# Slot mixture on one core: one stacked matmul per output tile, with the slot weights prepared ahead of the second expert layer

## The chip, the cores and the metric

One Trainium2 chip, one of its cores. The metric is the device time of one execution in microseconds; a change is judged by the medians of runs of both kernels on the same chip.

## The reference

Attention over learned states feeds a dense layer pair, and that feeds a soft mixture of experts, whose end is what the change touches. `x` has 4608 tokens (8 batches of 512 tokens and 32 state rows) of 512 features, `phi` has 32 slots, 4 for each of 8 experts.

```python
logits = x @ phi                                  # 4608 x 32
d = softmax(logits, axis=0)                       # over the tokens
slot_input = (d.T @ x).reshape(8, 4, 512)
for e in range(8):
    h = np.maximum(slot_input[e] @ w1[e], 0.0)    # 512 -> 1024
    slot_out[e] = h @ w2[e]                       # 1024 -> 512
c = softmax(logits, axis=1)                       # over the slots
return (c @ slot_out.reshape(32, 512)).astype(np.float32)
```

## The kernel before, in words

Eight batches `b` run through attention and the dense layers, and a ninth block `B` holds the 256 state rows. For each the kernel keeps its logits, transposed, in `LT` (512 tokens a batch, in 128 columns) or `LTs` (the state rows). After the last block comes the tail, from line 864 on. It takes the slot inputs (`SI`), the first expert layer (lines 900 to 912: 16 weight slices of 1 MB, 64 matmuls into two PSUM tiles `h1`), and then what the change touches:

- **csoft** (lines 660 to 677) turns the logits in `LT` into the softmax weights of the slots: transpose, maximum, subtraction, exponential, sum, reciprocal, a multiplication on POOL, transpose back.
- **csplit** (lines 679 to 688) spreads these weights for the output matmuls. `pick` (lines 916 to 918) selects one token tile of 128 and copies its 32 slot rows into 64 output rows, so that two batches lie one above the other in a PSUM tile `X` of 128 rows. ScalarE rounds both copies to `fp32r` (a float32 read at reduced precision by TensorE, in one pass), and DVE puts the rounding remainder into the first 32 rows of each 64. Four tiles `LC`, one for each pair of batches, and one `LCs`.
- **hTD** (lines 924 to 934): the first layer's output, transposed and laid on a block diagonal.
- **slot_out(dh)** (lines 943 to 961), for each half `dh` of 256 output columns: for each expert, 8 float32 matmuls with 32 stationary columns, which write four 32-row strips of `SO`. Then the four strips are summed by a matmul with `R` (which also repeats the 32 slot rows four times) into `SR`. ScalarE writes its rounding, DVE the remainder, to `so[0]` and `so[1]`. `SO` and `SR` share one PSUM buffer (pool `psE`, tag `E`).
- **combine(dh)** (lines 963 to 988): nine blocks, in the order 0 to 5, B, 6, 7, with 4 token tiles (2 for B), 34 a half. A tile is two `fp32r` matmuls (line 975), one against `so[0]` (rounding and remainder of the weights at once) and one against `so[1]`. DVE and ScalarE take turns at the eviction; even tiles lie in the three buffers of `psH`, odd ones in the two of `psX`, which `csplit` and `hTp` use as well. A block's 512 KB leave by one DMA on SP's queue; those of B by 8 small ones from POOL.

Lines 990 to 999 set the order of emission: `slot_out(0)` whole, then the splits, then `slot_out(1)` and `combine(0)` in turns by the string `CFG["so"]` (`s` is one expert, `c` one block), then what is left of both and `combine(1)`. A scheduler at build makes the order on each engine from this: of the instructions whose inputs its own estimate has ready, it takes the one emitted first. `group` (lines 121 to 129) keeps a list of matmuls together in that order, by putting all but the first 2000 places forward.

SBUF places are handed on by `give` and `take`: as soon as a weight slice is used up, its place gets the next load (all on SP's queue in this stretch). Four places of the first layer's slices are kept back (`kept`, line 900) for `ct`, `LC`, `hTD` and `so`, in this order. `so` is zeroed by four DVE instructions (lines 936 to 940).

Of the kernel before, what the change touches and what calls it, by code (L numbers as in the profile page):

```python
# [7 lines left out]
F32 = mybir.dt.float32  # L8
F32R = mybir.dt.float32r
U32 = mybir.dt.uint32  # L10
ACTF = mybir.ActivationFunctionType
ALU = mybir.AluOpType
# [1 line left out]
PSUM = bass.MemoryType.PSUM  # L14


CFG = dict(hp=2000, att7=(3, 5, 6, 7, 8, 10), og=1, n3=1, n3m=10, wS=['DP', 'AD', 'AD', 'AD', 'AD', 'DP', 'AD', 'DD', 'AD', 'AD', 'AD', 'AD', 'AD', 'AD', 'AD', 'AD'], xsm=13, k0=5, rg=6, spg=0, att0=6, att=7, V0=(2, 6, 10), Vn=(0, 4, 10), Vx=12, wn='H', wsev='adad', conv=(4, 8, 9, 11, 12, 13, 19, 21, 24, 26, 28, 32, 36, 40, 44, 48, 52, 56, 60), todo=[1, 1, 1, 2, 0, 0, 0, 3, 0, 0, 2, 2, 1, 1, 0, 0], E0=2, E=1, sm=1, tqB=(5, 9, 13), GP=10, pe=(3,), psH=3, gtpX=(0, 7), tq0=(13, 15), keep=(2, 3, 4, 5), x2=(1, 1), natm=1, warm=14, bounce7=(0, 3), split=1, wt=4, so='ssccsccccccsss', smm=(1, 2, 3, 4, 5, 6, 9), tqv=(), tqvm=0, first='x', apath=2, f32c=1, place=1, attm=(3, 6, 7, 8, 9, 12), subPm=True, loDm=False, bounce=(0, 1, 2, 3), bq=('s', 's'), xq='s', nat=((1, 11), (2, 2), (2, 3), (2, 11), (3, 2), (3, 4), (3, 9), (4, 2), (4, 3), (4, 9), (5, 2), (5, 3), (5, 9), (6, 2), (6, 4), (6, 9)), subP=(1,), mulD=(), loD=(), qlag=0, gv0='EEEEEEEEEEEEEEEE', gv='EEEEEEEEEEEEEEEE', gvS='BBBBBBBBBBBBBBBB')


@with_exitstack  # L20
def kernel(
# [14 lines left out]
    nc = tc.nc  # L36
    B = xs.shape[0]
    NS = 32 * B
    scale = 0.125
# [5 lines left out]
    const = pool("const", 1)  # L45
# [4 lines left out]
    small = pool("small", 2)  # L50
    psH = pool("psH", CFG["psH"], space=PSUM)
    psE = pool("psE", 1, space=PSUM)
    psV = pool("psV", 1, space=PSUM)
    psX = pool("psX", 5 - CFG["psH"], space=PSUM)
    dram = pool("dram", 1, space=bass.MemoryType.DRAM)

    cst_t = const.tile([128, 260], F32, name="cst_t")
    ident = cst_t[:, 0:128]
    R = cst_t[:, 128:256]
    R4 = cst_t[:, 128:160]  # L60
    blk = cst_t[:, 256:260]
# [8 lines left out]
    wp = const.tile([128, NM, 32], F32, name="wp", tag="wp")  # L70
    XS = const.tile([128, 4, NS], F32, name="XS", tag="XS")
    acc = const.tile([128, 2048], F32, name="acc", tag="acc")
    NL = (B + 1) // 2
    LT = const.tile([128, 128 * B], F32, name="LT")
    LTs = const.tile([64, 128], F32, name="LTs")
    spare = const.tile([128, 1024], F32, name="spare", tag="spare")
    eS = const.tile([128, 512], F32, name="eS", tag="eS")
# [38 lines left out]
    mm = nc.tensor.matmul  # L116
# [4 lines left out]
    def group(calls, after=()):  # L121

        first = mm(**calls[0])  # L123
        for i in after:
            tc.add_manual_dep(first.ins, i.ins.name, SYNC, reason="side by side")
        with tc.high_priority(CFG["hp"]):
            for c in calls[1:]:
                e = mm(**c)  # L128
                tc.add_manual_dep(e.ins, first.ins.name, ORDER, reason="side by side")

    def act(out, in_, func=ACTF.Copy, **kw):
        return nc.scalar.activation(out=out, in_=in_, func=func, **kw)  # L132
# [258 lines left out]
    def ntok(b):  # L391
        return 512 if b < B else NS

    wS = {}
# [281 lines left out]
                                op=ALU.mult)  # L676
        nc.vector.transpose(out=L, in_=t)

    def csplit(parts, C):

        np_ = 64 * len(parts)
        X = psX.tile([128, 512], F32, tag="X", name="cX")[0:np_, 0:C.shape[1]]
        for q, (L, n) in enumerate(parts):
            for t in range(n // 128):
                mm(out=X[64 * q:64 * q + 64, 128 * t:128 * t + 128], lhsT=pick[0:n // 4, t, :], rhs=L, start=True, stop=True)
        act(C, X)
        for p in range(32, np_, 64):
            nc.vector.tensor_tensor(out=C[p:p + 32], in0=X[p:p + 32], in1=C[p:p + 32], op=ALU.subtract)

    def diag(t, stride, nk, first):  # L690

# [9 lines left out]
    def take(place, name, dt=F32):  # L701

        ts = [p.tile([128, n], dt, name=name, tag=tag) for p, tag, n in place]
        return ts, [t[:, c:c + 512] for t in ts for c in range(0, t.shape[1], 512)]
# [82 lines left out]
    todo = [lambda i=i: conv_win(i) for i in range(2, 8)] + [lambda i=i: conv_wo(i) for i in range(8, 16)]  # L787

    sm = None
    vg = None  # L790
    for b in range(B + 1):
# [6 lines left out]
        for m in range(NM):  # L798
# [12 lines left out]
            if b == 1 and m == CFG["E0"]:  # L811
                for k in range(4):
                    estep(0, k)
                sm = smblock(0)
            if b > 0 and m % 4 == CFG["E"]:
                if m >= 4:
                    estep(b, m // 4 - 1)
                elif b > 1:
                    estep(b - 1, 3)
                    sm = smblock(b - 1)  # L820
# [46 lines left out]
    sm = smblock(B)  # L867
# [13 lines left out]
    tail4 = run["tail"].rearrange("p (a k x) -> p a k x", a=4, k=4)  # L881
# [3 lines left out]
    for i in range(4):  # L885
        for jj in range(4):
            mm(out=SI[32 * jj:32 * jj + 32, :], lhsT=PT[:, jj, 32 * i:32 * i + 32],
               rhs=where["wo", i][1][jj], start=(i == 0), stop=(i == 3))
# [11 lines left out]
    kept, got = [], 0  # L900
    h1 = [psX.tile([128, 512], F32, tag="X", name=f"h1_{i}") for i in range(2)]
    for i in range(16):
        e, hf = divmod(i, 2)
        place, w = where["w1", i]
        for kt in range(4):
            mm(out=h1[hf][32 * kt:32 * kt + 32, :], lhsT=XD[e // 4][:, kt, 32 * (e % 4):32 * (e % 4) + 32], rhs=w[kt],  # L906
               start=(e == 0), stop=(e == 7))
# [5 lines left out]

    ct_place = kept.pop(0)
    ct, = take(ct_place, "ct")[0]
    pick = tail4[:, 1, 0:2].rearrange("p a (b x) -> p (a b) x", b=2)
    for t in range(4):
        nc.vector.tensor_scalar(out=pick[:, t, :], in0=R[:, 0:64], scalar1=blk[:, t:t + 1], scalar2=None, op0=ALU.mult)
    csoft(LTs, 128, 64, SIs)
    csoft(LT, 128 * B, 128, ct)  # L920
    free.append(ct_place)
    LC = take(kept.pop(0), "LC", F32R)[1]
    LCs = const.tile([64, 256], F32R, tag="wp", name="LCs")
    hTD_t, = take(kept.pop(0), "hTD")[0]
    hTD = hTD_t.rearrange("p (k x) -> p k x", k=8)
    nc.gpsimd.memset(hTD, 0.0)
    hTp = psX.tile([128, 8, 32], F32, tag="X", name="hTp")
    for hf in range(2):
        s = run["tail"][:, 1536 * (1 - hf):1536 * (1 - hf) + 512]
# [3 lines left out]
    act(diag(hTD_t, 256, 8, 0),  # L933
        hTp.rearrange("p k (e i) -> p k e i", i=4), ACTF.Relu)

    so = take(kept.pop(0), "so", F32R)[1]
    for t in so:
        nc.vector.tensor_scalar(out=t.rearrange("p (a b) -> p a b", a=2),
                                in0=cst_t[:, 0:256].unsqueeze(1).to_broadcast([128, 2, 256]),
                                scalar1=0.0, scalar2=None, op0=ALU.mult)  # L940
    so = [so[0:2], so[2:4]]

    def slot_out(dh):
        dc = slice(256 * dh, 256 * dh + 256)
        SO = psE.tile([128, 256], F32, tag="E", name="SO")
        for e in range(8):
            place, w = where["w2", 8 * dh + e]
            for ft in range(8):
                c = 32 * (ft % 4)
                mm(out=SO[c:c + 32, :], lhsT=hTD[:, ft, 32 * e:32 * e + 32],  # L950
                   rhs=w[ft // 2][:, 256 * (ft % 2):256 * (ft % 2) + 256], start=(e == 0 and ft < 4), stop=(e == 7 and ft >= 4))
            give(place)
            yield
        SOs = run["tail"][:, 1024 + 256 * dh:1280 + 256 * dh]
        act(SOs, SO)
        SR = psE.tile([128, 256], F32, tag="E", name="SR")
        mm(out=SR, lhsT=R, rhs=SOs, start=True, stop=True)
        for q in range(2):
            p, p2 = slice(64 * q, 64 * q + 64), slice(64 * q, 64 * q + 32)
            act(so[0][q][p, dc], SR[p])  # L960
            nc.vector.tensor_tensor(out=so[1][q][p2, dc], in0=SR[p2], in1=so[0][q][p2, dc], op=ALU.subtract)

    def combine(dh):
        dc = slice(256 * dh, 256 * dh + 256)
        n_ev = 0
        for b in list(range(B - 2)) + [B, B - 2, B - 1]:
            T = ntok(b) // 128
            place = next(p for p in free if p[0][2] >= 256 * T)
            free.remove(place)
            o = take(place, "o")[0][0][:, 0:256 * T].rearrange("p (t d) -> p t d", t=T)  # L970
            for t in range(T):
                q, p, L = (b % 2, slice(0, 128), LC[b // 2]) if b < B else (0, slice(0, 64), LCs)
                ps = (psH, psX)[n_ev % 2].tile([128, 256], F32, tag="HX"[n_ev % 2], name="ops")
                for i in range(2):
                    mm(out=ps, lhsT=L[p, 128 * t:128 * t + 128], rhs=so[i][q][p, dc], start=(i == 0), stop=(i == 1))  # L975
                if n_ev % 2:
                    act(o[:, t, :], ps)
                else:
                    nc.vector.tensor_copy(out=o[:, t, :], in_=ps)  # L979
                n_ev += 1  # L980
            if b < B:
                dma(out=out[544 * b:544 * b + 512, dc].rearrange("(t p) d -> p t d", p=128), in_=o)
            else:
                for bb in range(B):
                    t, q = divmod(bb, 4)
                    (nc.gpsimd.dma_start if CFG["og"] else dma)(out=out[544 * bb + 512:544 * bb + 544, dc], in_=o[32 * q:32 * q + 32, t, :])  # L986
            free.append(place)
            yield

    drain(slot_out(0))  # L990
    csplit([(LTs, NS)], LCs)
    for i in range(NL):
        csplit([(LT[:, 128 * b:128 * b + 128], 512) for b in range(2 * i, min(2 * i + 2, B))], LC[i])
    s1, c0 = slot_out(1), combine(0)
    for x in CFG["so"]:
        step(s1 if x == "s" else c0)
# [42 lines left out]
```

## Time and profile before

| | us |
|---|---|
| median of 3 runs (lowest to highest) | 540.88 (540.31 to 540.95) |
| the profiled execution, its own time | 540.54 |
| its span in the profile | 537.7 |
| TensorE matmuls busy | 481.8 (90% of the span) |
| DVE busy | 395.4 (74%) |
| ScalarE busy | 256.0 (48%) |
| POOL busy | 239.8 (45%) |

How to read it: the span is what the profiler saw from the first to the last instruction; the execution's own time lies 2.84 us above it. The shares are means over stages that differ, so the stage around the change is read on its own below. In the rows, PE is TensorE, PEld its weight loads, DVE VectorE, ACT ScalarE, POOL GpSimd, SPq and POOLq queues that issue DMAs; L950 is line 950. ACT shows L132, the line of its helper, and groups of matmuls show L123 and L128. A float32 matmul leaves two records, an `fp32r` one leaves one.

### The profile page before, as it was taken

Reading aid. Unit: us, or ns where it says so; the run is one execution under the profiler, and the core shown is the slowest. Engines: PE = TensorE matmul, PEld = TensorE weight load, DVE = VectorE, ACT = ScalarE, POOL = GpSimd, SP = SyncE. Lnnn points to the kernel's source line nnn. Section 1 sums busy time; section 2 is a strip of 40 time slices with the busy share of each in tenths; the row PEclk is TensorE's granted clock in tenths of the full one; section 3 lists DMA queues with packets and bytes.
Section 4 is the critical chain, followed back from the end, with each engine's and each line's share of the span. In section 5 each row is a group of like instructions: output and inputs, shape, how many; then the busy total and the mean of one; then the engine's idle time right before and its main releaser. Section 6 shows DMA issues by size and latency. Waiting matters only on the chain.

```text
span 537.7 us, 9910 instructions
## 1 busy us (share of the span) xinstructions
PE 481.8 (90%) x3757; PEld 273.0 (51%) x3757; DVE 395.4 (74%) x728; ACT 256.0 (48%) x508; POOL 239.8 (45%) x230
## 2 busy tenths in 40 slices
PE   4476999999987999999999999999997997999992
PEld 2132455665534555455455455456466683356481
DVE  2999989777578679969969979977964762345260
ACT  2343476576555456456455455455444462023152
POOL 0775667665317366465555555646471000110032
PEclk9686799999999999999999999999998999899996
DMA  8998082457378488789789878879797988996379
GB/s 314 419 402 325 1 293 100 157 177 197 117 227 322 110 296 289 240 251 276 283 219 274 276 222 265 285 221 349 260 324 217 364 338 306 388 419 249 118 254 294
DMA packets 40223, 140.30 MB, mean 261 GB/s; under 512 B 4336, under 2 KB 12912, under 8 KB 28272
## 3 DMA queue, kind: packets, MB, share of 16 engines
q1 hardware_dynamic: 38496, 131.81, 71.2%
q0 software_dynamic: 1680, 7.87, 4.4%
q8 instruction: 29, 0.48, 0.3%
q14 instruction: 18, 0.15, 0.1%
HBM read 98.24 MB, written 39.32 MB: 256 GB/s over the span
## 4 chain that ended last, share of the span: by engine, by line
PE 60%; DVE 18%; DMA 13%; ACT 3%; issue 2%; SPq 2%; POOL 0%; POOLq 0%; DVEq 0%; ACTq 0%
PE h L434 22%; PE F L123 5%; DMA gdr<-gD 4%; PE E L123 4%; PE V L123 4%; PE SO L950 4%; DMA nat<-gD 4%; PE h L442 4%; DMA nat<-gdr 3%; PE ops L975 3%; PE h L906 3%; DVE win L160 3%; PE gtp L512 2%; DVE win L158 2%; DVE v L384 2%
## 5 line engine op out<-in xcount | busy, mean ns | idle before, releaser
L434 PE MATMUL h<-a,v 128*128 128x512 f32 x744 | 200.3, 412 | 5.0 <-DVE nat L486 2.2
L464 POOL TENSOR_TENSOR c<-c 128x512 f32<-128x512 f32 x128 | 135.6, 1064 | 100.4 <-ACT c L132 99.9
L434 PEld LDWEIGHTS h<-a,v 128*128 128x128 f32 x744 | 133.9, 191 | 85.1 <-issue 28.2
L132 ACT ACTIVATE c<-h,half 128x512 f32<-128x512 f32 x128 | 87.8, 688 | 99.1 <-PE h L434 66.6
L486 DVE SCALAR_TENSOR_TENSOR g<-h,c 128x512 f32<-128x512 f32 x112 | 75.2, 672 | 29.8 <-POOL c L464 29.7
L521 DVE STREAM_TRANSPOSE gD<-g 128x512 f32<-128x512 f32 x108 | 75.6, 703 | 1.6
L132 ACT ACTIVATE v<-V 128x512 fp32r<-128x512 f32 x62 | 37.0, 597 | 29.5 <-DVE v L384 14.8
L384 DVE TENSOR_TENSOR v<-V,v 128x512 fp32r<-128x512 f32 x62 | 42.1, 679 | 10.5 <-ACT v L132 9.7
L123 PE MATMUL V<-win,st_t 64*32 64x512 f32 x64 | 35.1, 629 | 9.8 <-POOL win L168 6.5
L128 PE MATMUL V<-win,st_t 64*32 64x512 f32 x448 | 38.3, 630 | 0.0
L123 PE MATMUL F<-nat,dN 128*32 128x512 f32 x54 | 26.9, 601 | 4.5 <-DMA nat<-gdr 2.9
L123 PE MATMUL E<-g,wp 128*32 128x512 f32 x56 | 29.2, 604 | 0.7 <-DVE g L486 0.7
L128 PE MATMUL E<-g,wp 128*32 128x512 f32 x168 | 29.6, 604 | 0.0
L128 PE MATMUL F<-nat,dN 128*32 128x512 f32 x162 | 27.2, 601 | 0.0
L986 POOL DMA_DIRECT2D out_dram<-o x16 | 7.9, 501 | 42.8 <-DVE o L979 37.2
L442 PE MATMUL h<-XSh,v 128*128 128x256 f32 x128 | 26.4, 298 | 0.2 <-ACT nat L132 0.2
L979 DVE COPY o<-ops 128x256 f32<-128x256 f32 x34 | 13.6, 423 | 15.8 <-PE ops L975 15.4
L623 DVE SCALAR_TENSOR_TENSOR acc<-acc,al,F 128x512 f32<-128x512 f32 x28 | 20.7, 739 | 5.7 <-PE F L128 5.5
L320 POOL TENSOR_TENSOR a<-att,a 128x512 fp32r<-128x512 f32 x14 | 18.1, 1305 | 13.4 <-ACT a L132 13.4
L975 PE MATMUL ops<-so,LC 128*128 128x256 f32 x128 | 23.3, 308 | 0.2
L442 PEld LDWEIGHTS h<-XSh,v 128*128 128x128 f32 x128 | 21.2, 197 | 4.1 <-issue 1.9
L264 POOL TENSOR_TENSOR att<-att,m 128x512 f32<-128x512 f32 x14 | 15.1, 1081 | 18.3 <-DVE m L263 15.6
(239 smaller groups left out, 780.9 us busy)
## 6 DMA issues: line engine op xcount, KB each, us to landing
gdr<-gD SPq DMA_DIRECT2D x100, 256.0 KB, 4.8
nat<-gdr SPq DMA_DIRECT2D x25, 1024.0 KB, 5.5
w<-in_w_dram SPq DMA_DIRECT2D x24, 1024.0 KB, 8.8
xn<-in_xn_dram SPq DMA_DIRECT2D x8, 1024.0 KB, 7.7
out_dram<-o SPq DMA_DIRECT2D x16, 512.0 KB, 5.4
xs<-in_xs_dram SPq DMA_DIRECT2D x7, 1024.0 KB, 7.7
w<-in_w_dram POOLq DMA_DIRECT2D x5, 1024.0 KB, 9.5
wb<-in_win_dram SPq DMA_DIRECT2D x4, 1024.0 KB, 11.7
```

The source lines that it names most:

```text
L123: first = mm(**calls[0])
L128: e = mm(**c)
L132: return nc.scalar.activation(out=out, in_=in_, func=func, **kw)
L384: nc.vector.tensor_tensor(out=lo[:, G, :], in0=V[G], in1=hi[:, G, :], op=ALU.subtract)
L434: mm(out=h, lhsT=v[:, G, f], rhs=a[:, G, :], start=(k == 0), stop=(k == 5))
L442: mm(out=h, lhsT=w[:, j, :], rhs=x[:, j, :], start=(k == 0), stop=(k == 11))
L464: nc.gpsimd.tensor_tensor(out=c, in0=c, in1=c, op=ALU.mult)
L486: gI[b, m] = nc.vector.scalar_tensor_tensor(out=g, in0=h, scalar=1.0, in1=c, op0=ALU.max, op1=ALU.min)
L521: nc.vector.transpose(out=gd[:, :, :, m4, :].rearrange("p c a i -> p a c i"), in_=gT[b, m].rearrange("p (a c i) -> p a c i", a=4, i=32))
L623: nc.vector.scalar_tensor_tensor(out=a, in0=a, scalar=al, in1=F, op0=ALU.mult, op1=ALU.add)
L950: mm(out=SO[c:c + 32, :], lhsT=hTD[:, ft, 32 * e:32 * e + 32], rhs=w[ft // 2][:, 256 * (ft % 2):256 * (ft % 2) + 256], start=(e == 0 and f ...
L975: mm(out=ps, lhsT=L[p, 128 * t:128 * t + 128], rhs=so[i][q][p, dc], start=(i == 0), stop=(i == 1))
```

## The change

Three things, and a new order string (an entry of `CFG`, line 17).

1. Each batch has its own weights tile of 128 rows: rounding in rows 0 to 31, remainder in 32 to 63, rounding again in 64 to 95 and in 96 to 127. The slot rows are one tile: rounding in rows 0 to 63, remainder in 64 to 95, zeros in 96 to 127. One matmul over all rows gives the three products of a token tile. `pick` has 128 columns instead of 64. The additional weights tiles lie in the place of `eS` and in three quarters of the place of `so`.
2. The splits are emitted ahead of `hTD` and of the second layer; `hTD` takes the last of the four kept places instead of the third.
3. The 8 matmuls of an expert in `slot_out` are emitted as a `group`. The zeroing of `so` is gone; a ScalarE write with scale 0 makes the zero rows.

```diff
-so='ssccsccccccsss'
+so='cscscscscscscscs'
...
-    def csplit(parts, C):
-        np_ = 64 * len(parts)
-        X = psX.tile([128, 512], F32, tag="X", name="cX")[0:np_, 0:C.shape[1]]
-        for q, (L, n) in enumerate(parts):
-            for t in range(n // 128):
-                mm(out=X[64 * q:64 * q + 64, 128 * t:128 * t + 128], lhsT=pick[0:n // 4, t, :], rhs=L, start=True, stop=True)
+    def csplit(L, n, C):
+        X = psX.tile([128, 512], F32, tag="X", name="cX")[:, 0:n]
+        for t in range(n // 128):
+            mm(out=X[:, 128 * t:128 * t + 128], lhsT=pick[0:n // 4, t, :], rhs=L, start=True, stop=True)
         act(C, X)
-        for p in range(32, np_, 64):
-            nc.vector.tensor_tensor(out=C[p:p + 32], in0=X[p:p + 32], in1=C[p:p + 32], op=ALU.subtract)
+        nc.vector.tensor_tensor(out=C[32:64], in0=X[32:64], in1=C[32:64], op=ALU.subtract)
...
-    LC = take(kept.pop(0), "LC", F32R)[1]
-    LCs = const.tile([64, 256], F32R, tag="wp", name="LCs")
+    LC = take(kept.pop(0), "LC", F32R)[1] + [const.tile([128, 512], F32R, tag="eS", name="LCe")]
+    so = take(kept.pop(0), "so", F32R)[1]
+    LC += so[1:]
+    so = so[0]
+    LCs = const.tile([128, 256], F32R, tag="wp", name="LCs")
+    for b in range(B):
+        csplit(LT[:, 128 * b:128 * b + 128], 512, LC[b])
+    csplit(LTs, NS, LCs)
     hTD_t, = take(kept.pop(0), "hTD")[0]
...
-            for ft in range(8):
-                c = 32 * (ft % 4)
-                mm(out=SO[c:c + 32, :], lhsT=hTD[:, ft, 32 * e:32 * e + 32],
-                   rhs=w[ft // 2][:, 256 * (ft % 2):256 * (ft % 2) + 256], start=(e == 0 and ft < 4), stop=(e == 7 and ft >= 4))
+            group([dict(out=SO[32 * (ft % 4):32 * (ft % 4) + 32, :], lhsT=hTD[:, ft, 32 * e:32 * e + 32],
+                        rhs=w[ft // 2][:, 256 * (ft % 2):256 * (ft % 2) + 256],
+                        start=(e == 0 and ft < 4), stop=(e == 7 and ft >= 4)) for ft in range(8)])
...
-        for q in range(2):
-            p, p2 = slice(64 * q, 64 * q + 64), slice(64 * q, 64 * q + 32)
-            act(so[0][q][p, dc], SR[p])
-            nc.vector.tensor_tensor(out=so[1][q][p2, dc], in0=SR[p2], in1=so[0][q][p2, dc], op=ALU.subtract)
+        act(so[0:96, dc], SR[0:96])
+        act(so[96:128, dc], SR[96:128], scale=0.0)
+        nc.vector.tensor_tensor(out=so[64:96, dc], in0=SR[64:96], in1=so[64:96, dc], op=ALU.subtract)
...
-                for i in range(2):
-                    mm(out=ps, lhsT=L[p, 128 * t:128 * t + 128], rhs=so[i][q][p, dc], start=(i == 0), stop=(i == 1))
+                mm(out=ps, lhsT=L[:, 128 * t:128 * t + 128], rhs=so[:, dc], start=True, stop=True)
```

## Rows read from the trace of the kernel before

**Rows 1.** The head of the page.

```profile
span 537.7 us, 9910 instructions
```

**Rows 2.** Windows: stretch, us, busy PE, PEld, DVE, ACT, POOL; PEclk, DMA share, GB/s.

```profile
477.40:485.00 7.60, 7.60 (x133) 4.43 (x132) 1.66 (x2) 0.76 (x2) 0.60 (x1) 1.00 1.02 414
485.00:490.30 5.30, 4.71 (x55) 3.99 (x51) 2.96 (x5) 1.96 (x4) 0.00 (x0) 1.00 1.02 422
493.00:513.50 20.50, 20.50 (x169) 9.59 (x168) 7.04 (x16) 3.45 (x9) 2.04 (x4) 1.00 0.30 96
513.50:536.00 22.50, 14.24 (x93) 11.98 (x92) 8.72 (x22) 10.45 (x28) 5.87 (x12) 0.84 0.96 310
530.00:536.00 6.00, 0.00 (x0) 0.00 (x0) 0.00 (x0) 0.00 (x0) 0.00 (x0) 0.50 1.05 345
```

**Rows 3.** Timeline of SP's queue, merged: start, us, what; the last weight loads.

```profile
431.91 45.33 SPq L714 DMA_DIRECT2D w<-in_w_dram  x23
```

**Rows 4.** The chain that ended last, in order of time: start, us, what.

```profile
478.01 7.06 PE SO L950 x128
...
490.35 0.43 PE ops L975 x2
490.78 1.51 PE cX L685 x16
...
493.07 1.86 PE SO L950 x32
...
499.12 0.56 PE SO L950 x4
499.68 0.43 PE ops L975 x2
...
512.99 0.55 PE SO L950 x2
...
515.12 2.17 PE ops L975 x15
```

**Rows 5.** The same chain: matmuls with 128 stationary columns.

```profile
447.17 1.09 PE warm L574 x8
...
475.54 1.90 PE hTp L932 x16
```

**Rows 6.** Groups from 475 to the end, shapes apart: busy us, mean ns of one.

```profile
L979 DVE COPY o<-ops 128x256 f32<-128x256 f32 x34 | 13.6, 423 | 15.8 <-PE ops L975 15.4
L132 ACT ACTIVATE o<-ops 128x256 f32<-128x256 f32 x34 | 12.8, 383 | 20.4 <-PE ops L975 19.5 <-DMA out_dram<-o 0.2
...
L688 DVE TENSOR_TENSOR LC<-cX,LC 32x512 fp32r<-32x512 f32 x8 | 5.5, 690 | 8.1 <-ACT LC L132 8.0
...
L132 ACT ACTIVATE LC<-cX 128x512 fp32r<-128x512 f32 x4 | 2.4, 597 | 4.1 <-PE cX L685 4.1
```

**Rows 7.** Timeline of the tail: start, us, engine, line, operation.

```profile
468.74 1.81 POOL L926 MEMSET hTD<- 128x2048 f32 x1 [7.26 <-DMA w<-in_w_dram]
...
470.27 1.55 DVE L938 TENSOR_SCALAR so<-cst_t 128x512 fp32r<-128x512 f32 x4
...
478.03 1.25 DVE L677 STREAM_TRANSPOSE LT<-ct 128x1024 f32<-128x1024 f32 x1 [2.08 <-POOL ct L675]
...
492.44 0.42 DVE L961 TENSOR_TENSOR so<-SR,so 32x256 fp32r<-32x256 f32 x1
...
496.91 0.40 SPq L982 DMA_DIRECT2D out_dram<-o  x1
...
513.58 0.38 ACT L132 ACTIVATE tail<-SO 128x256 f32<-128x256 f32 x1 [1.16 <-PE SO L950]
...
515.15 0.38 ACT L132 ACTIVATE so<-SR 64x256 fp32r<-64x256 f32 x1
```

**Rows 8.** DMA view of 497 to 502 in 40 slices: busy tenths.

```profile
DMA  0000001899999999998200000000000000000000
```

**Rows 9.** Windows, as rows 2, over the slot inputs and the first layer.

```profile
450.00:460.00 10.00, 7.12 (x64) 2.71 (x60) 2.69 (x10) 1.68 (x5) 0.52 (x1) 1.00 0.79 276
460.00:470.00 10.00, 10.00 (x80) 3.09 (x81) 3.02 (x6) 0.21 (x1) 1.65 (x2) 0.83 1.02 428
```

More of the change, by code (lines that the diff above doesn't have):

```diff
@@ L14 @@
 PSUM = bass.MemoryType.PSUM
-CFG = dict(hp=2000, att7=(3, 5, 6, 7, 8, 10), og=1, n3=1, n3m=10, wS=['DP', 'AD', 'AD', 'AD', 'AD', 'DP', 'AD', 'DD', 'AD', 'AD', 'AD', 'AD', 'AD', 'AD', 'AD', 'AD'], xsm=13, k0=5, rg=6, spg=0, att0=6, att=7, V0=(2, 6, 10), Vn=(0, 4, 10), Vx=12, wn='H', wsev='adad', conv=(4, 8, 9, 11, 12, 13, 19, 21, 24, 26, 28, 32, 36, 40, 44, 48, 52, 56, 60), todo=[1, 1, 1, 2, 0, 0, 0, 3, 0, 0, 2, 2, 1, 1, 0, 0], E0=2, E=1, sm=1, tqB=(5, 9, 13), GP=10, pe=(3,), psH=3, gtpX=(0, 7), tq0=(13, 15), keep=(2, 3, 4, 5), x2=(1, 1), natm=1, warm=14, bounce7=(0, 3), split=1, wt=4, so='ssccsccccccsss', smm=(1, 2, 3, 4, 5, 6, 9), tqv=(), tqvm=0, first='x', apath=2, f32c=1, place=1, attm=(3, 6, 7, 8, 9, 12), subPm=True, loDm=False, bounce=(0, 1, 2, 3), bq=('s', 's'), xq='s', nat=((1, 11), (2, 2), (2, 3), (2, 11), (3, 2), (3, 4), (3, 9), (4, 2), (4, 3), (4, 9), (5, 2), (5, 3), (5, 9), (6, 2), (6, 4), (6, 9)), subP=(1,), mulD=(), loD=(), qlag=0, gv0='EEEEEEEEEEEEEEEE', gv='EEEEEEEEEEEEEEEE', gvS='BBBBBBBBBBBBBBBB')
+CFG = dict(hp=2000, att7=(3, 5, 6, 7, 8, 10), og=1, n3=1, n3m=10, wS=['DP', 'AD', 'AD', 'AD', 'AD', 'DP', 'AD', 'DD', 'AD', 'AD', 'AD', 'AD', 'AD', 'AD', 'AD', 'AD'], xsm=13, k0=5, rg=6, spg=0, att0=6, att=7, V0=(2, 6, 10), Vn=(0, 4, 10), Vx=12, wn='H', wsev='adad', conv=(4, 8, 9, 11, 12, 13, 19, 21, 24, 26, 28, 32, 36, 40, 44, 48, 52, 56, 60), todo=[1, 1, 1, 2, 0, 0, 0, 3, 0, 0, 2, 2, 1, 1, 0, 0], E0=2, E=1, sm=1, tqB=(5, 9, 13), GP=10, pe=(3,), psH=3, gtpX=(0, 7), tq0=(13, 15), keep=(2, 3, 4, 5), x2=(1, 1), natm=1, warm=14, bounce7=(0, 3), split=1, wt=4, so='cscscscscscscscs', smm=(1, 2, 3, 4, 5, 6, 9), tqv=(), tqvm=0, first='x', apath=2, f32c=1, place=1, attm=(3, 6, 7, 8, 9, 12), subPm=True, loDm=False, bounce=(0, 1, 2, 3), bq=('s', 's'), xq='s', nat=((1, 11), (2, 2), (2, 3), (2, 11), (3, 2), (3, 4), (3, 9), (4, 2), (4, 3), (4, 9), (5, 2), (5, 3), (5, 9), (6, 2), (6, 4), (6, 9)), subP=(1,), mulD=(), loD=(), qlag=0, gv0='EEEEEEEEEEEEEEEE', gv='EEEEEEEEEEEEEEEE', gvS='BBBBBBBBBBBBBBBB')
 @with_exitstack
@@ L72 @@
     acc = const.tile([128, 2048], F32, name="acc", tag="acc")
-    NL = (B + 1) // 2
     LT = const.tile([128, 128 * B], F32, name="LT")
@@ L915 @@
     ct, = take(ct_place, "ct")[0]
-    pick = tail4[:, 1, 0:2].rearrange("p a (b x) -> p (a b) x", b=2)
+    pick = tail4[:, 1]
     for t in range(4):
-        nc.vector.tensor_scalar(out=pick[:, t, :], in0=R[:, 0:64], scalar1=blk[:, t:t + 1], scalar2=None, op0=ALU.mult)
+        nc.vector.tensor_scalar(out=pick[:, t, :], in0=R, scalar1=blk[:, t:t + 1], scalar2=None, op0=ALU.mult)
     csoft(LTs, 128, 64, SIs)
@@ L934 @@
         hTp.rearrange("p k (e i) -> p k e i", i=4), ACTF.Relu)
[L936 to L941, printed above, removed]
     def slot_out(dh):
@@ L971, in combine @@
             for t in range(T):
-                q, p, L = (b % 2, slice(0, 128), LC[b // 2]) if b < B else (0, slice(0, 64), LCs)
+                L = LC[b] if b < B else LCs
                 ps = (psH, psX)[n_ev % 2].tile([128, 256], F32, tag="HX"[n_ev % 2], name="ops")
-                for i in range(2):
-                    mm(out=ps, lhsT=L[p, 128 * t:128 * t + 128], rhs=so[i][q][p, dc], start=(i == 0), stop=(i == 1))
+                mm(out=ps, lhsT=L[:, 128 * t:128 * t + 128], rhs=so[:, dc], start=True, stop=True)
                 if n_ev % 2:
@@ L990 @@
     drain(slot_out(0))
-    csplit([(LTs, NS)], LCs)
-    for i in range(NL):
-        csplit([(LT[:, 128 * b:128 * b + 128], 512) for b in range(2 * i, min(2 * i + 2, B))], LC[i])
     s1, c0 = slot_out(1), combine(0)
```

## The prediction

> **What bounds the kernel now.** I read the page's head first, then the windows over the tail, then the chain of waits and the timeline there; everything that the diff touches runs after 467 us of a 537.7 us span [rows 1]. That execution took 540.54 us, 2.84 more than its span and 0.34 less than the median of the runs shown, 540.88. My sum is a difference to the span, set against the median.
>
> The windows cut the tail into stages [rows 2]. From 477.4 to 485 TensorE is full and the DMA engines are full as well, at 414 GB/s: these are the last weight loads, all issued by 477.3 on SP's queue [rows 3], so nothing that starts later can delay one. From 493 to 513.5 TensorE is busy all the time while DMA stands at 0.30 and 96 GB/s. From 513.5 to 536 DMA is at 0.96, and its last 6 us, at 345 GB/s, have no other work beside them. The output is 9.44 MB (4608 x 512 x 4 bytes); from 513.5 to 536 the queues move 22.5 x 310 = 7.0 MB, so less than 2.5 MB of it had gone by then. So the kernel ends on an output queue that was fed too late, and it was fed late because TensorE was the bound from 493 to 513.5. The last 1.7 us follow the last transfer.
>
> The chain shows why TensorE takes 20.5 us there [rows 4]. The first strips of the second layer (64 calls, 128 records, since a float32 call leaves two) run as one piece in 7.06 us, 0.88 per expert: four 32-column strips share the array. Between 493 and 513.5 the other half's 64 calls are cut into pieces between token tiles. A piece of 4 records takes 0.56 us, while four calls side by side (8 records) are 0.44 in the whole run, so a cut strip pays for four calls when it does two; the chain has 19 such pieces from 493.07 to 513.54, 12.4 us together. A token tile's two matmuls take 0.43 beside a piece, but 0.29 in the run of 15 in 2.17 (0.145 each). A round of one tile and one piece therefore costs 0.14 for the tile and, against those 0.44, 0.12 for the piece more than the same work in runs: about 0.26, say 0.27, for a change over and back.
>
> **The change part by part.**
>
> *Split of the slot weights.* The number of calls stays (32 for the eight blocks and 2 for the states), but each has 128 stationary columns instead of 64, and all go ahead of the second layer. Sixteen records of 64 columns took 1.51 us, 94 ns each [rows 4]. No call of this shape is in the trace; the nearest with 128 stationary and 128 moving columns is the warming one, eight records in 1.09 us, 136 ns [rows 5]. The transposing step to hTp has 128 stationary and only 32 moving columns: 119 ns [rows 5]. So 64 records cost 6.0 to 8.7 us; I take 125 ns, 8.0 us, between the last two, as these are alike in what they load. The Trainium skill, TensorEngine Tiling (Array Packing), Theoretical Speedup, speaks against this edit: a stationary side of at most 64 columns can run two at a time, up to twice as fast, which the new form gives up. By that rule 64 records would cost twice 94 ns, 12.0 us, and the sum below would end 4 us later, near 537; the 136 ns of a full-width record speak against it. ScalarE's evictions of the split grow from 4 to 8 of 0.60 us, DVE's subtractions stay 8 of 0.69 [rows 6]. With two PSUM buffers one block can be split every (1.0 + 0.60 + 0.69 + 0.1) / 2 = 1.2 us; TensorE fills the gaps with strips, which need other PSUM.
>
> *Order.* The weights are there at 479.3, after the last transpose on DVE [rows 7]. The four zeroings (1.55 us on DVE, between two steps of that softmax) vanish, so they should come about 1.5 us earlier, at 477.8, beside hTD at 478.0. That is worth nothing by itself: TensorE has strips to do from 478.0 on. The clearing of hTD on POOL moves to the place that the zeroings had and waits for what they waited for: start 470.3 instead of 468.74, 1.81 us long, done 6 us before the last transpose, whose input POOL multiplies just ahead of it [rows 7]. No DMA is moved past another on SP, and POOL's output DMAs keep their place behind the last copies.
>
> *Strips as groups.* First half: 8 x 0.88 = 7.06 us. With eight splits of 1.0 us and four changes to and fro (two splits for each strip, as two buffers allow) at 0.27, TensorE is done at 478.0 + 7.06 + 8.0 + 1.1 = 494.2. The changes could be 0 to 8 (0 to 2.2 us).
>
> *From strips to slot rows.* One eviction, one matmul, two ScalarE writes, one subtraction. The second half of before shows them almost undisturbed: eviction at 513.58, first slot row written at 515.53 [rows 7]. The zeroed rows cost another 0.38 beside DVE's 0.42. I take 2.0 us for the first half, where TensorE is free: slot rows at 496.2. TensorE has nothing else in that gap, since the second half's strips wait for the one PSUM buffer that holds these rows: in before they start at 493.07 on the chain, as soon as DVE's last subtraction from it has ended at 492.86 [rows 4, 7]. Before, the first token tile could start at 490.3, but the strips at 493.1; now both start at 496.2. These 3.2 us are the price of moving the split ahead.
>
> *Combining.* 34 token tiles a half (8 x 4 + 2) take one matmul instead of two, 34 x 0.145 = 4.9 us of TensorE saved a half. Evictions stay at 0.42 on DVE and 0.38 on ScalarE alternately [rows 6], some 0.22 a tile: 7.5 us a half. With five PSUM buffers, four to five tiles go between two strips. A round is 0.88 + 4.25 x 0.145 + 0.27 = 1.77 us, eight rounds 14.1: strips and first half end at 510.3, where before the strips ended at 513.5 with 10 tiles still to do (169 records from 493 on less the strips' 128, and 7 ahead of them on the chain, make 48, 24 tiles of 34). A round moves 4.25 x 131 KB, 315 GB/s, just below the 345 of the output queue. Bounds: with all strips first 8 x 0.88 = 7.1 us, and one change more in each round 16.3.
>
> *The end.* Second slot rows: +2.2 us, 512.5. First block of the second half: four tiles, issue and start of the transfer. In before the first output is issued at 496.91 [rows 7]; four tiles at 0.22 and some latency make 1.2, and from issue to data it is 0.9 (the engines start in the slice from 497.75) [rows 8]: 514.6. The first half's 4.72 MB start at 496.2 + 2.1 = 498.3 and at 345 GB/s are gone at 512.0, so little of them is left. The second half's 4.72 MB at 345 take 13.7: 528.3, and 1.7 to the end of the span: 530.0. That is 7.7 us less than 537.7. From the median: 540.88 - 7.7 = 533.2; I round to **533.0 us**.
>
> **The rivals.**
>
> *The output queue is the floor.* If the scheduler leaves fewer tiles between strips, the second slot rows come before 510 and the queue never runs dry: 498.3 + 27.4 + 1.7 = 527.4, a time of 530.6. For it: a backlog of two blocks at 512 (1.5 us each at 345 GB/s) would bridge the hole. Against: 315 GB/s in a round leaves none.
>
> *The grouping doesn't hold, or the splits come late.* The order on an engine is made at build from estimated times. If strips are still cut, they cost 12.4 instead of 7.1 us in the second half: 5.3 later, 538.3. If the eight splits run without strips between them, at 1.2 us each, it is 1.6 us later, 534.6.
>
> *TensorE's clock: slower than before.* From 450 to 460 TensorE is busy 7.12 of 10 us, and in the next 10 us, busy throughout, its granted clock is 0.83: about a third of them at 1.2 GHz [rows 9]. The new gap before 496.2 and the thinner matmuls might bring that about in the rounds. A third of 10 us at the lower level is 1.7 us of work: 534.7. If all eight rounds ran at 1.2 GHz, their 12.0 us of matmuls would double: slot rows at 524.5, time 545.0, slower. It decides from about 8 us of added TensorE time on, two thirds of the rounds. Against it: 485 to 490.3, where TensorE is not full either (4.71 of 5.3), has 1.00 [rows 2], and the gap is short. The Trainium skill, TensorE: Matmul & The Clock Gate, Part 1, states the rule behind this rival: the low clock is the default and only sustained activity lifts it. The trace agrees in the 0.50 of the idle window at the end [rows 2].
>
> **How the numbers follow.** Forecast (531.5 to 536) 0.57; floor 0.22; cut strips or a late split beyond 536 0.12; clock throughout, or any other way to the slow side, 0.05; nothing to be seen 0.04. The time is that of the forecast. With every term at its low end (splits 6.0, no changes) the first slot rows come 3.1 us sooner and the queue's floor holds: 527.5. At the high end, splits 8.7, eight changes and 16.3 for the rounds, the second slot rows come 4 us later, 537; with cut strips it is 538.3. I give 528.0 to 538.5. A change of 0.2%, 1.1 us, is about what a measurement of this kernel can tell from none. Faster by more 0.91, within 0.04, slower 0.05.
>
> **What would show it.** Right: the strips' records in runs of 16 or more at 0.88 a strip; 68 matmuls of token tiles; DMA at 300 GB/s or more from 499 on; the end still on the output queue. Each split record at 120 to 136 ns. Wrong: strips in pieces of 2 to 8; splits at 190 ns; a granted clock below 1 between 496 and 511; first output after 500; a hole in the DMA share of more than 3 us around 512.

## The result, and the profile after

The changed kernel takes 544.50 us (median of 6, 542.29 to 545.61) against 540.83 us of the kernel before in the same comparison: a ratio of 1.0075, interval 1.0051 to 1.0100. It is slower, on the side on which the prediction had put 1 chance in 20, and outside its range. The profiled execution took 544.80 us with a span of 543.0.

The chain that ended last, in order of time (start, us, what), from the moment the slot weights are ready:

```profile
477.12 1.26 DVE LT L676
478.37 0.14 issue
478.51 3.63 PE cX L682 x16
482.14 0.02 issue
482.16 0.61 ACT LC L131
482.76 0.02 issue
482.79 0.69 DVE LC L684
483.48 0.04 issue
483.53 1.17 PE cX L682 x8
...
491.21 2.88 PE hTp L934 x16
...
494.16 0.39 ACT hTD L131
...
503.95 0.39 ACT tail L131
...
506.40 0.73 PE ops L967 x4
507.14 0.33 PE SO L122
...
508.14 0.31 PE ops L967
...
518.17 0.80 PE ops L967 x5
```

The transposing step `hTp` of the second layer's input, which in before ran at 475.54, ahead of any split of the batches [rows 5], now stands behind all of them. Each split needs a PSUM tile that ScalarE and DVE have cleared (0.61 + 0.69 us), so with two tiles a pair of blocks takes 2.56 us (483.53 to the next pair at 486.09), longer than the 2.0 us of its matmuls at full clock. Only after the last one comes `hTp`, 15.7 us later than before. No strip can start before `hTD`, so nothing else runs on TensorE meanwhile. The first strips run from 494.60 to 503.87 (before: 478.01, [rows 4]), and the first token tile is made at 506.40 (before: 490.35).

The windows of after (us, busy PE, PEld, DVE, ACT, POOL, PEclk, DMA share, GB/s) show two consequences:

```profile
475.00:480.00 5.00, 2.45 (x19) 1.57 (x12) 1.28 (x2) 1.19 (x2) 1.91 (x1) 0.84 1.01 420
480.00:485.00 5.00, 4.59 (x31) 4.34 (x31) 2.05 (x3) 2.07 (x4) 0.00 (x0) 0.82 1.03 415
485.00:490.00 5.00, 4.19 (x33) 3.66 (x32) 2.73 (x4) 2.26 (x5) 0.00 (x0) 1.00 1.01 421
490.00:495.00 5.00, 3.71 (x24) 3.19 (x27) 1.02 (x2) 1.21 (x3) 0.00 (x0) 0.71 0.44 184
495.00:500.00 5.00, 5.00 (x64) 2.43 (x60) 0.00 (x0) 0.00 (x0) 0.00 (x0) 0.61 0.02 3
500.00:505.00 5.00, 4.43 (x74) 2.19 (x66) 0.00 (x0) 0.38 (x1) 0.00 (x0) 1.00 0.00 0
505.00:510.00 5.00, 3.69 (x44) 2.01 (x47) 1.68 (x5) 1.61 (x5) 0.00 (x0) 1.00 0.24 79
510.00:515.00 5.00, 5.00 (x70) 2.41 (x62) 1.52 (x4) 1.34 (x4) 0.00 (x0) 1.00 0.40 135
```

The granted clock is 0.84 and 0.82 where the splits begin, 1.00 in the middle of them, and falls to 0.71 and 0.61 behind them; before had 1.00 in each of its windows of that stretch [rows 2]. And the queues stand still from 495 to 505. The first output is issued at 507.96 (before: 496.91, [rows 7]), and all 9.44 MB still have to leave.

### The profile page after: what moved, and what is told of

Read it like the earlier page. It is cut to its first block, busy times and chain, and to the rows that moved or that the text cites. A ratio compares the mean times of both kernels' runs of the same rounds, so it can differ in the third digit from the quotient of the medians.

```text
span 543.0 us, 9765 instructions
## 1 busy us (share of the span) xinstructions
PE 477.0 (88%) x3689; PEld 272.2 (50%) x3689; DVE 391.8 (72%) x722; ACT 257.2 (47%) x512; POOL 239.7 (44%) x230
## 4 chain that ended last, share of the span: by engine, by line
PE 56%; DVE 22%; DMA 11%; ACT 4%; issue 3%; POOL 1%; SPq 1%; POOLq 0%; DVEq 0%; ACTq 0%
PE h L433 20%; PE F L122 5%; PE E L122 4%; DMA nat<-gD 4%; DMA gdr<-gD 4%; PE V L122 4%; PE h L441 3%; DMA nat<-gdr 3%; DVE win L159 3%; DVE gD L520 2%; DVE win L157 2%; PE gtp L511 2%; PE ops L967 2%; DVE v L383 2%; DVE g L485 2%
## 5 line engine op out<-in xcount | busy, mean ns | idle before, releaser
L167 POOL TENSOR_TENSOR win<-win,LT 128x512 uint32<-128x512 uint32 x7 | 12.8, 1835 | 22.2 <-DVE win L159 17.3
L285 POOL TENSOR_TENSOR att<-att,z 128x512 f32<-128x512 f32 x16 | 17.3, 1086 | 10.0 <-DVE z L284 6.8
```

The costliest lines, as they stand in the source:

```text
L285: (nc.vector if b in CFG["mulD"] else nc.gpsimd).tensor_tensor(out=t3, in0=t3, in1=z1.unsqueeze(2).to_broadcast([128, 16, 32]), op=ALU.mult)
```

## The experiments

Each ratio is to the kernel before on the same chip. That kernel's medians were 538.56 us in the comparison of the first four runs below and 538.91 in that of the last three, from 534.2 to 542.3 us. A ratio can lie up to 0.2% off the quotient of the two medians; the ratios with their intervals carry the verdicts.

### hTp in the PSUM buffer of SO and SR

```diff
-    hTp = psX.tile([128, 8, 32], F32, tag="X", name="hTp")
+    hTp = psE.tile([128, 8, 32], F32, tag="E", name="hTp")
```

> One word changed: the tile hTp lies in the buffer of SO and SR instead of one of the two that the splits use; the order of emission stays that of the change. Theory A (hTp queues behind all nine splits for their two PSUM buffers, so that hTD and with it every strip of the second layer comes 16 us late): hTp is done by 478, strips lie between the splits, first slot rows at 496 to 497 instead of 506, first output by 499, and the time is 531 to 535. Theory B (the splits, paced by their two buffers at 1.3 us a block and at 146 ns a record, hold up the strips by themselves wherever hTp is): the splits still end at 490, the first strips run behind them, slot rows not before 502, time 540 to 544. Theory C (the half clock of 490 to 499 is the cost): it goes only if the holes go; under A the granted clock is 1.00 from 480 to 515, under B it is still below 0.85 somewhere there.

535.52 us, ratio 0.9928 (0.9900 to 0.9956): faster than before, where the change as given is slower. The chain, as above:

```profile
478.91 2.02 PE cX L682 x16
480.93 0.33 PE SO L122
...
483.66 1.98 PE cX L682 x16
...
488.37 1.98 PE cX L682 x16
...
492.21 2.00 PE cX L682 x16
...
496.05 0.62 PE ops L967 x3
...
497.67 0.31 PE ops L967
...
498.99 0.55 PE ops L967 x3
...
507.70 0.79 PE ops L967 x5
```

Theory A holds for everything up to the slot rows. Three, three and two strips lie between the pairs of splits, the first tile is at 496.05 (forecast: 496.2), and the clock is 1.00 from 480 to 515: its dips are gone together with the waits. Theory B falls: the splits still take 8.0 us of TensorE, but strips lie between them. One part of A missed: the first output is issued at 499.75, not by 499, the time lies just past its 531 to 535, and the gain is 0.7%, not the 1.4% of the prediction. The chain shows why. Of the first block, three tiles come ahead of the first strip and the fourth behind it; in all only 17 of the 34 tiles are made when the strips end at 507.70, and 22 with the five right behind them.

### The splits behind the first strips, as they stood before

```diff
+    drain(slot_out(0))
     for b in range(B):
         csplit(LT[:, 128 * b:128 * b + 128], 512, LC[b])
     csplit(LTs, NS, LCs)
...
-    drain(slot_out(0))
```

> The changed kernel with the nine splits emitted behind the first half of the second layer, where they stood before; one matmul a tile, groups and the order string stay. Theory A: hTp is free again, the first half's strips run from 478 to 485 in one piece, slot rows at about 488, splits lie among the second half's strips, and the first output leaves at 490 to 493, ahead of e2: 529 to 534, and as the output queue is then the floor, within 3 us of e2. Theory B: with the splits out of the way of the first half, this one is clearly faster than e2, by 6 us or more.

536.64 us, ratio 0.9963 (0.9928 to 0.9998). `hTp` is free here too, and theory B's 6 us are not there: it is no faster than the run before this. But theory A's early output is not there either, and the time is past its 529 to 534. The first tile is made at 490.76, and yet the first output is issued at 504.94. ScalarE's timeline (start, us, line, operation, idle time before it) has the reason:

```profile
490.80 0.60 ACT L131 ACTIVATE LCe<-cX 128x512 fp32r<-128x512 f32 x1 [0.30 <-PE cX L682]
495.30 0.60 ACT L131 ACTIVATE so<-cX 128x512 fp32r<-128x512 f32 x1 [3.90 <-PE cX L682]
496.20 0.60 ACT L131 ACTIVATE so<-cX 128x512 fp32r<-128x512 f32 x1 [0.30 <-PE cX L682]
499.51 0.60 ACT L131 ACTIVATE so<-cX 128x512 fp32r<-128x512 f32 x1 [2.72 <-PE cX L682]
501.51 0.38 ACT L131 ACTIVATE LCs<-cX 128x256 fp32r<-128x256 f32 x1 [1.40 <-PE cX L682]
...
504.26 0.66 ACT L131 ACTIVATE o<-ops 128x256 f32<-128x256 f32 x2
```

It evicts no odd tile before 504.26. Odd tiles lie in the same two PSUM buffers as the splits and are emitted behind them, so here it is the tiles that stand behind the splits. That reads as the same queue as in the changed kernel, with another victim; it is read from the timeline and the code, and no run moves the odd tiles to show it.

### The groups alone

The kernel before, with only this from the diff:

```diff
-            for ft in range(8):
-                c = 32 * (ft % 4)
-                mm(out=SO[c:c + 32, :], ...)
+            group([dict(out=SO[32 * (ft % 4):32 * (ft % 4) + 32, :], ...) for ft in range(8)])
```

> The kernel before with only the grouping of an expert's 8 matmuls; two matmuls a tile, splits and order string of before. If a cut strip costs what the prediction said (12.4 against 7.1 us in the second half), the stretch from 493 to the second slot rows is 5 us shorter and the time 535 to 537. If whole strips only delay the token tiles behind them, the stretch and the time stay: 540 to 541.

533.71 us, ratio 0.9891 (0.9851 to 0.9931): 1.1%, 5.9 us on that run's 538.56 (the medians themselves are 4.9 apart), against the 5.3 us that the prediction gave to uncut strips. The time is on the side of the first theory, and below its 535 to 537. By the chain the second half's strips start at 492.01, and behind them come these:

```profile
504.48 1.77 PE ops L974 x10
506.25 0.43 PE SR L956 x2
```

That is 12.5 us from 492.01 to 504.48, where before had 20.5 [rows 2]; a part of the difference is tiles that are now made later, as fewer lie between the strips. This one part is ahead of the whole change, even with `hTp` freed, though those two intervals overlap.

### hTp freed, without the groups

The first experiment with the old loop over `ft`.

> e2 without the grouping: hTp in its own buffer, splits ahead, one matmul a tile, but the strips' matmuls free to be cut. Against e2 it prices the groups under the new form: if cut strips cost the 5 us of the prediction, 536 to 540; if a tile of one matmul leaves the scheduler little to cut with, within 2 us of e2.

542.25 us, ratio 1.0053 (1.0018 to 1.0088), 1.25% or 6.7 us above the same kernel with groups; more than the 5 us named, past the 536 to 540, and on the side of that theory. The second half's strips are cut into pieces of 2 to 16 records, mostly by single tiles at 0.31 us. Without groups, the one matmul a tile and the splits ahead make the kernel slower than before even when `hTp` is not in the queue.

### Four tiles between two strips

The first experiment, with an order edge:

```diff
     def group(calls, after=()):
         first = mm(**calls[0])
+        if "tile" in run:
+            tc.add_manual_dep(first.ins, run["tile"].ins.name, ORDER, reason="behind the block")
...
-                mm(out=ps, lhsT=L[:, 128 * t:128 * t + 128], rhs=so[:, dc], start=True, stop=True)
+                run["tile"] = mm(out=ps, lhsT=L[:, 128 * t:128 * t + 128], rhs=so[:, dc], start=True, stop=True)
```

> e2 (hTp in its own buffer) with one order edge more: no strip of the second half starts on TensorE before the last token tile emitted ahead of it, so four to five tiles lie between two strips as the prediction had it, where e2 has 1 to 3. Theory A2 (after hTp is freed, what is left of the gap to the prediction is a thin feed of the output queue: only 22 of the 34 tiles of the first half were done when e2's strips ended): the first output leaves at 497 to 498 instead of 499.75, the strips end 1 to 2 us later than in e2, but all but one or two tiles are done by then, and the time is 3 to 4 us below e2, 0.985 to 0.988 of the kernel before. Theory B2 (the output queue moves no more than e2 gave it, whatever order feeds it): as e2, 0.992 to 0.994.

530.53 us, ratio 0.9843 (0.9803 to 0.9883). This is theory A2, just past the end of its bracket, and the lowest ratio of all runs, though its interval overlaps those of the groups alone and of the last run. Chain and windows:

```profile
497.50 0.85 PE ops L969 x5
...
499.36 0.67 PE ops L969 x4
...
501.03 0.67 PE ops L969 x4
...
509.37 0.55 PE ops L969 x3
```

```profile
500.00:505.00 5.00, 5.00 (x62) 2.93 (x61) 2.48 (x8) 1.85 (x7) 0.00 (x0) 1.00 0.95 318
505.00:510.00 5.00, 5.00 (x64) 2.77 (x66) 2.38 (x7) 1.81 (x6) 2.78 (x6) 1.00 0.93 302
```

A round of four tiles and a strip takes 1.67 us (499.36 to 501.03); 32 of 34 tiles are done when the strips end, and the output queue moves 302 to 318 GB/s where before had 96 from 493 on [rows 2]. The first output is issued at 499.07 rather than 497 to 498, because the whole tail of the profiled execution, at 532.91 us the slowest of the six, lies later: its slot weights are ready at 480.22 instead of 478.77 in the first experiment.

### The waits of the changed kernel filled

The changed kernel itself, `hTp` behind the splits, with matmuls on the identity where TensorE waits. They add work and change no result.

```diff
+    fw = psE.tile([128, 128], F32, tag="E", name="fill")
+    def fill(n):
+        for _ in range(n):
+            f = mm(out=fw, lhsT=ident, rhs=ident, start=True, stop=True)
+            tc.add_manual_dep(f.ins, run["pe"].ins.name, ORDER, reason="fill")
+    fill(8)
     for b in range(B):
         csplit(LT[:, 128 * b:128 * b + 128], 512, LC[b])
+        if b % 2:
+            fill(2)
```

(`run["pe"]` is the last matmul of the first layer or of the splits.)

> The changed kernel as it is, hTp behind the splits, with 16 idle matmuls on the identity that change no result: 8 between the first layer and the first split, 2 after every second split, where TensorE waits. Theory A (the wait for hTp costs by itself, the half clock comes on top): the granted clock is 1.00 from 476 to 505, hTp takes 1.9 instead of 2.9 us and the first strips 7.1 instead of 9.3, slot rows come 3 to 5 us sooner, at 501 to 503, the time is 1.000 to 0.996 of the kernel before. Theory C (the clock is the whole of the loss): 0.990 or less. If neither clock nor time changes, the holes did not lower the clock.

539.42 us, ratio 1.0007 (0.9975 to 1.0039). The clock is 1.00 again at the splits and still falls behind them; windows and chain:

```profile
480.00:485.00 5.00, 4.87 (x41) 4.49 (x40) 2.73 (x4) 2.26 (x5) 0.00 (x0) 1.00 1.04 424
485.00:490.00 5.00, 4.23 (x38) 3.58 (x41) 1.78 (x3) 1.76 (x4) 0.00 (x0) 0.97 1.01 416
490.00:495.00 5.00, 5.00 (x72) 2.73 (x68) 0.00 (x0) 0.00 (x0) 0.00 (x0) 0.69 0.28 115
```

```profile
475.94 1.14 PE cX L682 x8
...
487.05 1.99 PE hTp L944 x16
...
489.55 0.51 PE SO L122
...
498.91 0.71 PE SR L961 x2
...
500.93 0.74 PE ops L977 x4
```

From the first split to the first tile it is 24.99 us (475.94 to 500.93), where the changed kernel needs 27.89 (478.51 to 506.40). So 2.9 us of its delay went with the filled waits, and so did 0.7% of the time: theory A, and not theory C. The splits give 1.6 of it (11.11 us to the start of `hTp` instead of 12.70), `hTp` to the first strip 0.9 (2.50 instead of 3.39), the first strips 0.4. The clock still dips to 0.69 after 490, so those did not come down to 7.1 us, as expected, but only to about 8.9. The slot weights are ready 2.6 us sooner in this execution (475.80 instead of 478.38); the stretch from the first split leaves that out.

### The old form with groups and four tiles

The kernel before with the groups, the order string of the change and the order edge; two matmuls a tile, splits as in before.

> The kernel before with only the groups (as the run with the groups alone), the new order string and the order edge of four tiles between two strips; two matmuls a tile, packed splits behind the first strips. If an even feed of the output queue is what decides, its rounds of 0.88 + 4 x 0.29 + 0.27 = 2.3 us start at 492 and end at 510, the queue is fed from 491 on and the end comes 1 to 3 us before that of the groups alone: 0.983 to 0.988 of the kernel before. If the later second slot rows decide, it is 2 to 4 us behind the groups alone: 0.993 to 0.997.

531.12 us, ratio 0.9870 (0.9835 to 0.9906). Its first output is issued at 492.45, 4.5 us ahead of before, and its strips end at 507.93. The ratio lies inside the bracket of the first theory, 0.2% below that of the groups alone; the intervals overlap, so that step alone is not settled. Neither is whether one matmul a tile is worth anything: this form and the run with four tiles in the new form differ by 0.3%, with intervals of 0.8%.

## Why the prediction was wrong, point by point

**The step that failed** is the cover of the split: "TensorE fills the gaps with strips, which need other PSUM", and with it "That is worth nothing by itself: TensorE has strips to do from 478.0 on". The strips' own PSUM is free, but their input `hTD` comes out of `hTp`, and `hTp` lies in the two buffers of the splits and is emitted behind them. I had named the users of `psX` in the description and priced the two buffers as a pace (1.2 us a block; measured 1.28), but never as a queue with an order. The experiment that moves `hTp` alone to another buffer, with the order of emission kept, shows it.

From the first split to the first tile the changed kernel needs 27.89 us and the first experiment 17.14 (478.91 to 496.05). The 10.75 us between them, from the two chains:

- the splits from first to last, with nothing between them to cover their pace: 12.70 (478.51 to 491.21) instead of 7.98 (four pairs of 2.0): 4.72
- `hTp` and the eviction to `hTD` on the path, 491.21 to 494.60: 3.39
- first strips 9.27 instead of 7.32: 1.95
- slot rows 2.53 instead of the 1.84 that the last splits leave uncovered: 0.69

Some of the first three is the low clock (the first pair took 3.63 us, `hTp` 2.88 where before took 1.90 [rows 5]). Filling the waits gave back 2.9 us of it, and 1.5 more are left in the first strips of that run (8.85 against 7.32). So the clock comes to about 4.4 of the 10.75 us, and the waits for buffers and inputs to about 6.3. With `hTp` moved, and nothing else, the clock was 1.00 from 480 to 515, so its part goes with the queue as well.

**The second step that failed** is "With five PSUM buffers, four to five tiles go between two strips." In the first experiment the build put one to three there, so that 17 of 34 tiles were done when the strips ended. The buffers allowed more; its order did not use them. With the order edge, three to five lie ahead of each strip, the kernel gains another 0.85% (0.9928 to 0.9843), and 8 rounds take 13.5 us (497.50 to 510.96) against the forecast's 14.1.

**A smaller miss** is the term of 2.0 us for the slot rows. Where nothing covers them they took 2.53 (503.87 to 506.40): the write of the zero rows, which the prediction had beside DVE's subtraction, ends at 505.90, and the subtraction starts behind it at 505.92.

**What was right.** With both steps mended the kernel does what was forecast: 530.53 us, a ratio of 0.9843, where the prediction's 7.7 us are 0.986. Split records cost 125 ns (16 in 1.98 to 2.02 us), the value taken; twice the 94 ns of a 64-column record, 188 ns, is not seen. The first tile came at 496.05 against 496.2, and that close a match is partly luck: the splits started 0.9 us later than the 478.0 of the sum, and the changes between splits and strips cost about 0.3 us (strips 7.32 against 7.06) where it had 1.1. Cut strips cost 5.9 to 6.7 us against 5.3. The end stayed on the output queue, at 300 to 356 GB/s in the last window of 5 us in which it was full in each run.

**The rivals.** "The splits come late" was the right rival with a wrong price: 1.6 us, because I counted the pace of splits without strips and let the strips be ready meanwhile, which left out `hTp` and `hTD` on the path. The clock was right as a symptom, in another place (at the first splits and from 490 to 500, not in the rounds) and with about 4.4 us instead of 12. "Strips still cut" did not happen. A time on the slower side had 0.05; a queue in front of a shared buffer deserved more, since both halves of it were at hand: that `hTp` uses the splits' buffers, and that the diff puts it behind them.

## What to carry to other kernels

When a step is moved ahead of another, list the buffers that both use, not only the data. Here a tile that was emitted later in the same small pool stood behind all the earlier ones, and everything that reads it stood there too. A stage that "other work will cover" is covered only if that work's whole chain of inputs avoids the stage's buffers; check the chain back to the last thing that is ready. And fewer matmuls are not yet a gain when a queue ends the kernel: whole strips alone gave 1.1%, and fixing the number of tiles between them 0.85% with the new form, while a gain from one matmul a tile is not shown.

## What the runs showed of the hardware

I had not expected TensorE's clock to fall in a stretch in which the engine had so much to do: in the changed kernel it was busy 12.5 of the 15 us from 480 to 495. It fell twice, as finer windows show (columns as above):

```profile
477.50:480.00 2.50, 1.49 (x7) 1.52 (x8) 0.86 (x1) 0.00 (x0) 0.00 (x0) 0.69 1.01 421
480.00:482.50 2.50, 2.50 (x15) 2.47 (x15) 0.68 (x1) 0.94 (x2) 0.00 (x0) 0.63 1.03 410
485.00:487.50 2.50, 2.10 (x18) 1.87 (x17) 1.37 (x2) 1.13 (x3) 0.00 (x0) 1.00 1.02 423
492.50:495.00 2.50, 1.98 (x12) 1.65 (x15) 0.00 (x0) 0.38 (x1) 0.00 (x0) 0.50 0.04 16
```

The first dip stands behind 2.55 us in which TensorE waited for the slot weights (to 478.51), a wait that the kernel before fills with `hTp`. With matmuls put into it, the clock there was 1.00, and the first pair of splits took 2.02 us instead of 3.63. Between the splits themselves, with waits of 0.4 us after each pair, it was 1.00. The second dip, 0.50 from 492.5 to 497.5, stands behind waits of 0.77 and 0.52 us around `hTp`; with matmuls between the splits it still came, shorter (0.50 from 490 to 492.5, then 0.87), behind waits of 0.18 and 0.52 us. It made the first strips of the changed kernel 9.3 us long, for work of 7.1. In before, 485 to 490.3 with 4.71 us busy kept 1.00 [rows 2], so what brings the second dip stays open.

And a stationary side of 128 columns instead of 64 made a split record 1.33 times as long (125 against 94 ns), not twice.
